# Which DMA queue carries the raw MoE weights during attention, and how the absolute values of a block are spread over slots

## The chip, the cores and the metric

The kernel runs on one core of a Trainium2 chip. The metric is the device time of one execution in microseconds (us); the time of a kernel is the median of several runs.

## What is computed

The reference chains three stages, all in float32 at their ends:

```python
# 1. attention over 2 x 8 heads, 768 tokens, 64 wide: a token sees only tokens of its own cluster
mask = argmax(q_n @ c_n)[:, None] == argmax(k_n @ c_n)[None, :]
attn = softmax(where(mask, scale * q @ k.T, -1e9));  x = concat_heads(attn @ v)      # 1536 x 512
# 2. a dense block of 2048 hidden units; w_in and w_out arrive as float64
h = x @ w_in;  r = maximum(h, 0);  x = (s * r * r + b) @ w_out
# 3. eight experts, top-1 routing
e = argmax(x_n @ en.T / tau);  out = gate[:, None] * (maximum(x @ w1[e], 0) @ w2[e])
```

## The kernel before

Attention runs head by head, sixteen heads. The order of its instructions is written out by hand: every step is entered with a due time by `at(t, f)` (twelve units of due time to a head), the steps are sorted by due time, and `order.pin` keeps that order on all five engines: TensorE (PE), VectorE (DVE), ScalarE (ACT), GpSimd (POOL) and SyncE (SP, which only issues DMAs). So each engine, and the DMA queue that it feeds, meets its instructions in the order of the due times.

For each head, TensorE computes the maxima's scores (`M`, line 223, tile M), which VectorE reduces. `mneg` and `mrow` turn the row maxima of a head into one row: TensorE transposes them (line 235, tile mr), ScalarE copies the row out of PSUM (line 237, tile mrs), and SyncE issues a 3 KB DMA that writes the row into the head's tile qa (line 238, qa<-mrs). The next head's score products (`Sx`, line 247) read that row, so TensorE waits for the DMA before the first of them; ScalarE takes the exponentials (line 249) and TensorE multiplies with v (line 268).

Stage 2 needs w_in and w_out as float32. They arrive as float64 and are converted by bit operations, in 16 blocks f = 0 to 15. `load_f64(f, eng)` issues the two loads of a block, 512 KB each (lines 522 and 523, tile raw), on the queue of the engine `eng`. The tiles raw have six buffers, that is, three blocks. `conv_steps(f)` converts a block in steps: ScalarE takes absolute values of both halves (line 422), VectorE clamps (425), shifts (432) and merges sign and low bits (435 and 437, twice), and the last step issues the load of block f + 3 into the buffers that block f has left (line 441). The steps of blocks 0 to 3 are spread over three heads each, at the due times of `CONV` added to 36 f + 12. The steps of block 4 follow one unit apart from due time 176.2, during the last two heads. Blocks 0 to 2 are loaded at the due times of `FETCH` on ScalarE's queue.

Which block's load goes where, before: block 3 (issued behind the conversion of block 0) on ScalarE's queue; blocks 4, 5, 6 and 7 (issued behind the conversions of blocks 1, 2, 3 and 4) on SyncE's. The loads of blocks 8 to 15 are issued on SyncE's queue in stage 2, whose first chunk converts the remaining blocks.

The load behind the conversion of block f < 4 has due time 36 f + 43.2, which is unit 7.2 of a head. Around it in that head stand: the load of v (due 6), the two conversions of the coming k and q on ScalarE (6 and 8, line 150), the exponentials (7, 8, 9), and `mrow` (8.5).

Of the kernel before, what the change touches and what calls it, by code (L numbers as in the profile page):

```python
# [33 lines left out]
WARM = -26  # L34
HEAT = ((-41, 7), (-30.5, 6), (-22, 6))
SETUP, FETCH = 6.3, (5.3, 17.3, 29.3)
CONV = (3.2, 7.2, 11.2, 15.2, 19.2, 23.2, 27.2, 31.2)
F, DM, TC = 2048, 512, 512
NF, KD, NTT = F // P, DM // P, TC // P
E, F2 = 8, 1024  # L40
NWA = 5
# [339 lines left out]
class Moe:  # L381
# [11 lines left out]
    def hooks(self, ms, mb):  # L393
# [12 lines left out]
        for f in range(NWA):  # L406
            for n, t in enumerate(CONV):
                out.append((36 * f + 12 + t if f < NWA - 1 else 176.2 + n, lambda f=f: next(self.steps(f), None)))
# [7 lines left out]
    def conv_steps(self, f, wide=False):  # L416
        nc = self.nc
        r = self.loaded.pop(f)
        t = self.w32(f, U32)
        u = [self.ps([P, DM], "cv", "ab"[a]).bitcast(U32) if wide else t[:, a] for a in range(2)]  # L420
        for a in range(2):
            nc.scalar.activation(out=t[:, a].bitcast(F32), in_=r[a][:, :, 1].bitcast(F32), func=AF.Abs)
        yield
        s = t.rearrange("p a (w o) -> p o (a w)", o=2)
        nc.vector.tensor_scalar(out=s.bitcast(F32), in0=s.bitcast(F32), scalar1=CLAMP_LO, scalar2=CLAMP_HI, op0=ALU.max, op1=ALU.min)
        yield
        shift = dict(scalar1=5, scalar2=2, op0=ALU.logical_shift_left, op1=ALU.logical_shift_right)
        if wide:
            for a in range(2):
                nc.vector.tensor_scalar(out=u[a], in0=t[:, a], **shift)  # L430
        else:
            nc.vector.tensor_scalar(out=s, in0=s, **shift)
        yield
        for a in range(2):
            nc.vector.scalar_tensor_tensor(out=u[a], in0=r[a][:, :, 1], scalar=0xC0000000, in1=u[a], op0=ALU.bitwise_and, op1=ALU.bitwise_or)
            yield
            nc.vector.scalar_tensor_tensor(out=t[:, a], in0=r[a][:, :, 0], scalar=29, in1=u[a], op0=ALU.logical_shift_right, op1=ALU.bitwise_or)
            yield
        self.wT[f] = t
        if f + 3 < NF:  # L440
            self.loaded[f + 3] = self.load_f64(f + 3, nc.scalar if f + 3 < NWA - 1 else nc.sync)
        yield

    def pools(self):
# [747 lines left out]
```

## Time and profile before

| what | us |
|---|---|
| median of 3 runs | 823.32 |
| lowest and highest of the runs | 821.75, 825.11 |
| the profiled execution's own time | 824.21 |
| its span, first to last instruction | 822.3 |
| mean granted clock of TensorE, share of full speed | 0.967 |

The profile is of one execution. Times in its rows count from the first instruction of the span. A row of the timeline gives the start, the duration, the engine, the source line, the operation, the tile written and the tiles read, and in brackets the idle time of the engine just before it with what ended that. "SPq" and "ACTq" are the issuing queues of SyncE and ScalarE. A row of a window gives the stretch, its length, the busy time of each engine, the granted clock of TensorE and what the DMA engines did.

### The profile page before, as it was taken

What the parts mean: (1) busy time and instruction counts of PE and PEld (TensorE: products, weight loads), DVE (VectorE), ACT (ScalarE), POOL (GpSimd) and SP (SyncE); (2) the same over time, 40 slices, a digit from 0 to 9 for tenths busy, and PEclk for the clock granted to TensorE, in tenths of its full rate; (3) what the DMA queues carried; (4) which work ended last, traced back from release to release, by engine and by line L of the source; (5) the groups of instructions that cost most, each with busy time, mean ns of one, the idle gap of its engine ahead of it and who ended that gap; (6) DMA issues with size and microseconds to landing.
All of it is one profiled execution on the core that took longest, in us unless ns stands there. A gap on an engine that the chain in (4) does not pass through costs nothing. (4 is left out here: it accounts for less than half of the span.)

```text
span 822.3 us, 12229 instructions
## 1 busy us (share of the span) xinstructions
PE 769.7 (94%) x4191; PEld 580.2 (71%) x4193; DVE 526.9 (64%) x1087; ACT 421.6 (51%) x841; POOL 347.5 (42%) x277
## 2 busy tenths in 40 slices
PE   7699999898998889999999999997999999999994
PEld 3456555454554458888778787775879998989883
DVE  5769789695895779994353642648446635756650
ACT  5355465454653665646445554444346645756651
POOL 2067766575674655435434443445032202220000
PEclk9799999998998999999999999989999999999998
DMA  5155423334232205611000042254131844876600
GB/s 147 49 139 175 124 72 92 111 91 119 73 76 63 60 22 170 184 55 52 1 1 1 7 147 86 94 191 142 65 103 58 272 141 157 236 259 228 211 17 23
DMA packets 75470, 88.73 MB, mean 108 GB/s; under 512 B 7445, under 2 KB 58549, under 8 KB 75008
## 3 DMA queue, kind: packets, MB, share of 16 engines
q1 hardware_dynamic: 68704, 69.67, 27.9%
q0 software_dynamic: 4000, 13.90, 5.3%
q10 hardware_dynamic: 2688, 4.19, 1.7%
q8 instruction: 40, 0.66, 0.3%
q14 instruction: 38, 0.31, 0.1%
HBM read 70.57 MB, written 7.34 MB: 95 GB/s over the span
## 5 line engine op out<-in xcount | busy, mean ns | idle before, releaser
L531 POOL TENSOR_TENSOR wl<-w,wh 128x512 fp32r<-128x512 f32 x96 | 123.1, 1307 | 131.5 <-ACT wh L529 128.9
L249 ACT ACTIVATE pt<-S 128x384 f32<-128x384 f32 x192 | 91.6, 490 | 123.1 <-PE S L248 121.0
L224 DVE TENSOR_REDUCE mx<-M 128x1 f32<-128x384 f32 x192 | 101.8, 551 | 54.8 <-PE M L223 52.8
L260 POOL TENSOR_TENSOR acc<-acc,pt 128x768 f32<-128x768 f32 x61 | 106.1, 1740 | 6.5 <-ACT pt L249 4.1
L552 PE MATMUL hp<-x,wh 128*128 128x512 f32 x384 | 107.2, 400 | 0.3 <-ACT wh L529 0.3
L552 PE MATMUL hp<-x,spare 128*128 128x256 f32 x732 | 96.1, 284 | 2.0 <-PEq L984 1.7
L552 PEld LDWEIGHTS hp<-x,spare 128*128 128x128 f32 x732 | 92.7, 190 | 6.9 <-issue 4.1
L560 PE MATMUL y<-wd,gg 128*128 128x512 f32 x360 | 93.2, 395 | 0.0
L608 DVE SCALAR_TENSOR_TENSOR hp<-hp,sb,t 128x512 f32<-128x512 f32 x48 | 36.3, 757 | 78.8 <-ACT t L607 78.8
L247 PE MATMUL S<-qa,ka 97*128 97x384 f32 x192 | 72.5, 377 | 13.2 <-DMA qa<-mrs 11.5
L552 PEld LDWEIGHTS hp<-x,wh 128*128 128x128 f32 x384 | 71.9, 191 | 15.5 <-ACT wh L529 0.9
L223 PE MATMUL M<-ka,qa 80*128 80x384 f32 x192 | 79.0, 412 | 3.6 <-DVE mx L224 2.3
L268 PE MATMUL pv<-pt,vn 128*64 128x385 f32 x384 | 78.8, 534 | 0.0
L560 PE MATMUL y<-wh,gh 128*128 128x512 f32 x192 | 75.6, 394 | 1.7 <-ACT gh L611 1.7
L560 PE MATMUL y<-wl,gh 128*128 128x512 f32 x192 | 75.3, 392 | 0.0
L545 DVE TENSOR_TENSOR wd<-w,wd 128x512 fp32r<-128x512 f32 x64 | 43.3, 686 | 44.4 <-ACT wd L544 41.0
L560 PEld LDWEIGHTS y<-wd,gg 128*128 128x128 f32 x360 | 63.7, 189 | 10.1 <-DVE gg L1081 0.2
L1033 POOL DMA_INDIRECT row<-rows,idx x24 | 28.0, 1166 | 95.7 <-PE tp L1045 50.8
L248 PE MATMUL S<-qb,kb 128*128 128x384 f32 x192 | 66.7, 347 | 0.0
L607 ACT ACTIVATE t<-hp 128x512 f32<-128x512 f32 x48 | 28.7, 598 | 73.9 <-PE hp L552 73.9
L223 PEld LDWEIGHTS M<-ka,qa 80*128 80x128 f32 x192 | 37.1, 193 | 39.2 <-issue 8.2
L560 PE MATMUL y<-wh,gl 128*128 128x512 f32 x192 | 59.4, 391 | 0.0
(269 smaller groups left out, 1371.8 us busy)
## 6 DMA issues: line engine op xcount, KB each, us to landing
w<-in_moe_w_dram SPq DMA_DIRECT2D x128, 256.0 KB
raw<-in_moe_w_in_dram SPq DMA_DIRECT2D x12, 512.0 KB
raw<-in_moe_w_out_dram SPq DMA_DIRECT2D x12, 512.0 KB
qn<-in_q_dram SPq DMA_DIRECT2D x16, 192.0 KB
kn<-in_k_dram SPq DMA_DIRECT2D x16, 192.0 KB
vn<-in_v_dram SPq DMA_DIRECT2D x16, 192.0 KB
ka<-kb SPq DMA_DIRECT2D x16, 192.0 KB
qa<-qb SPq DMA_DIRECT2D x16, 192.0 KB
```

The costliest lines, as they stand in the source:

```text
L223: nc.tensor.matmul(pp, qa[i][0:80, r * P:(r + 1) * P], ka[i][0:80, c * HS:(c + 1) * HS])
L224: nc.vector.tensor_reduce(out=mxt[j % 2][:, r, c:c + 1], in_=pp, axis=AX.X, op=ALU.max)
L247: nc.tensor.matmul(pp, ka[i][0:97, t * P:(t + 1) * P], qa[i][0:97, w], start=True, stop=False)
L248: nc.tensor.matmul(pp, kb[i][:, t * P:(t + 1) * P], qb[i][:, w], start=False, stop=True)
L249: exps.setdefault((j, t), []).append(nc.scalar.activation(out=p[:, c, 0:HS], in_=pp, func=AF.Exp, scale=0.125).ins)
L260: eng.tensor_tensor(out=acc[j][-1], in0=acc[j][-1], in1=p[:, :, 0:HS], op=ALU.add)
L268: together(tc, [lambda c=c: nc.tensor.matmul(pv_t[j][c * 64:c * 64 + 64, :], io_t["v", j][:, t, :], p[:, c, :], start=t == 0, stop=t == NR ...
L531: eng.tensor_tensor(out=wl[:, a], in0=w[:, a], in1=wh[:, a].bitcast(F32), op=ALU.subtract)
L545: eng.tensor_tensor(out=t[:, 1], in0=w[:, a], in1=t[:, 0].bitcast(F32), op=ALU.subtract)
L552: self.nc.tensor.matmul(hp, a[:, k * P:(k + 1) * P], b(k), start=n == 0, stop=n == 3 * KD - 1)
L560: self.nc.tensor.matmul(y[i], (gl if n == 2 else gh)[:, s], wl if n == 1 else wh, start=first and n == 0, stop=last and n == 2)
L608: nc.vector.scalar_tensor_tensor(out=hp, in0=hp, scalar=sb[:, 0:1], in1=t, op0=ALU.mult, op1=ALU.mult)
```

## The change

The last step of a conversion chooses the queue by f instead of by f + 3, so that the loads of blocks 3, 4, 5 and 6 are issued on ScalarE's queue and only that of block 7 on SyncE's, among those issued during attention. The loads of blocks 8 to 15 stay on SyncE's. The two absolute values of a block, which were one step, become two steps; `CONV` gets one more due time, 5.2, for the second one. For block 4, whose steps are one unit apart, every step from the second absolute value on moves by one unit, and its last (the load of block 7) to 184.2.

```diff
-CONV = (3.2, 7.2, 11.2, 15.2, 19.2, 23.2, 27.2, 31.2)
+CONV = (3.2, 5.2, 7.2, 11.2, 15.2, 19.2, 23.2, 27.2, 31.2)
...
         for a in range(2):
             nc.scalar.activation(out=t[:, a].bitcast(F32), in_=r[a][:, :, 1].bitcast(F32), func=AF.Abs)
-        yield
+            yield
...
         if f + 3 < NF:
-            self.loaded[f + 3] = self.load_f64(f + 3, nc.scalar if f + 3 < NWA - 1 else nc.sync)
+            self.loaded[f + 3] = self.load_f64(f + 3, nc.scalar if f < NWA - 1 else nc.sync)
```

(NWA is 5.)

## Rows read from the trace of the kernel before

**Rows 1.** Page, part 1: busy time, share of the span and instructions of each engine.
```profile
PE 769.7 (94%) x4191; PEld 580.2 (71%) x4193; DVE 526.9 (64%) x1087; ACT 421.6 (51%) x841; POOL 347.5 (42%) x277
```

**Rows 2.** Windows of attention and of stage 2's first chunk: stretch, length, busy times, clock, DMA.
```profile
30.00:298.00 268.00, 245.88 (x1302) 145.04 (x1299) 207.81 (x434) 137.38 (x333) 163.38 (x108) 0.94 0.35 95
298.00:386.00 88.00, 87.75 (x386) 72.32 (x387) 74.94 (x121) 53.44 (x78) 47.04 (x36) 1.00 0.31 97
```

**Rows 3.** Timeline, TensorE: score products that waited for qa<-mrs, all five.
```profile
98.37 0.41 PE L247 MATMUL S<-qa,ka 97*128 97x384 f32 x1 [1.64 <-DMA qa<-mrs]
...
148.51 0.41 PE L247 MATMUL S<-qa,ka 97*128 97x384 f32 x1 [3.17 <-DMA qa<-mrs]
...
198.67 0.66 PE L247 MATMUL S<-qa,ka 97*128 97x384 f32 x1 [3.03 <-DMA qa<-mrs]
...
249.50 0.66 PE L247 MATMUL S<-qa,ka 97*128 97x384 f32 x1 [2.72 <-DMA qa<-mrs]
...
278.98 0.41 PE L247 MATMUL S<-qa,ka 97*128 97x384 f32 x1 [0.90 <-DMA qa<-mrs]
```

**Rows 4.** Timeline: issues of raw loads and of qa<-mrs, with mr and mrs before them.
```profile
92.20 0.41 ACTq L522 DMA_DIRECT2D raw<-in_moe_w_in_dram  x1
...
94.34 0.76 SPq L238 DMA_DIRECT2D qa<-mrs  x1
...
141.22 0.22 PE L235 MATMUL mr<-identr,mn 128*6 128x128 f32 x1
...
142.05 0.44 SPq L522 DMA_DIRECT2D raw<-in_moe_w_in_dram  x1
...
192.33 0.45 SPq L522 DMA_DIRECT2D raw<-in_moe_w_in_dram  x1
...
243.33 0.25 ACT L237 ACTIVATE mrs<-mr 6x128 f32<-6x128 f32 x1
243.48 1.35 SPq L522 DMA_DIRECT2D raw<-in_moe_w_in_dram  x1
...
245.48 0.75 SPq L238 DMA_DIRECT2D qa<-mrs  x1
...
277.06 0.73 SPq L238 DMA_DIRECT2D qa<-mrs  x1
```

**Rows 5.** Windows from one mr (line 235) to the next; columns as in Rows 2.
```profile
92.61:110.84 18.23, 16.38 (x87) 9.79 (x85) 11.68 (x27) 9.59 (x24) 10.47 (x8) 0.91 0.43 129
...
126.03:141.22 15.19, 14.84 (x86) 8.98 (x85) 14.21 (x30) 8.43 (x22) 11.14 (x8) 1.00 0.32 84
141.22:161.11 19.89, 16.50 (x86) 9.46 (x85) 11.68 (x27) 9.44 (x24) 10.44 (x8) 0.91 0.42 118
...
191.52:212.29 20.77, 17.53 (x87) 10.20 (x85) 11.68 (x27) 9.56 (x24) 10.43 (x8) 0.84 0.39 112
...
242.68:261.87 19.19, 16.05 (x67) 9.00 (x66) 11.65 (x27) 6.39 (x16) 8.57 (x5) 0.82 0.26 79
261.87:275.00 13.13, 12.63 (x64) 7.43 (x63) 8.05 (x17) 6.28 (x16) 8.57 (x5) 1.00 0.12 32
```

**Rows 6.** Timeline: ScalarE idle after block 1's absolute values; block 1's last merge.
```profile
109.84 0.49 ACT L249 ACTIVATE pt<-S 128x384 f32<-128x384 f32 x1 [1.40 <-PE S L248]
...
135.51 0.68 DVE L437 SCALAR_TENSOR_TENSOR w<-raw,w 128x512 uint32<-128x512 uint32 x1
```

**Rows 7.** Timeline: block 4's conversion near the end of attention, and who waits later.
```profile
275.65 1.25 ACT L422 ACTIVATE w<-raw 128x512 f32<-128x512 f32 x2
276.79 0.25 ACT L237 ACTIVATE mrs<-mr 6x128 f32<-6x128 f32 x1
276.93 0.70 DVE L425 TENSOR_SCALAR w<-w 128x1024 f32<-128x1024 f32 x1 [2.52 <-ACT w L422]
...
291.66 0.87 PE L284 MATMUL su<-acc,ones 128*64 128x384 f32 x4 [1.75 <-DVE xu L303]
```

**Rows 8.** Timeline, ScalarE's queue: the longest issue of a raw load.
```profile
73.78 2.43 ACTq L523 DMA_DIRECT2D raw<-in_moe_w_out_dram  x1
```

## The prediction

> **What bounds the kernel now.** I read the busy times on the page first: TensorE is busy 94% of the span [rows 1], so a change on queues can only be worth what TensorE idles or runs slow because of them. The windows by stage come next [rows 2]: attention (30 to 298 us) has 268.0 us with 245.9 us of TensorE at a granted clock of 0.94, and the first chunk of stage 2 right behind it is solid (87.75 of 88.0 us, clock 1.00). The reader is to see two things there. What attention loses is where this change acts, and what attention gains is handed on in full, since the stage behind it waits for nothing but its start.
>
> Then the list of TensorE's waits on DMAs. There is one kind in attention: the first score product of a head waits for the row qa<-mrs, five times, 11.46 us in all [rows 3]. Four of the five stand in the four heads in which a raw load is issued at unit 7.2; the fifth, 0.90 us, stands next to block 4's conversion. Last the issues [rows 4]: in each of the four heads the 1 MB of a raw block is issued just ahead of the small qa<-mrs (2.1 us in the first, 2.0 in the last), on ScalarE's queue in the first (92.20), on SyncE's in the other three (142.05, 192.33, 243.48).
>
> **What such a load costs.** From one mr to the next takes 15.19 us in a clean head (one row stands; six such lie between 15.18 and 15.21) [rows 5]. With a load it takes 18.23 us in the head with the load on ScalarE's queue, and 19.89, 20.77 and 19.19 us with it on SyncE's. So the first costs 3.04 us, the second 4.70, the third 5.58. The fourth has less work than a clean head, for there are no more heads to prepare: from its stalled product to the next mr it takes 12.37 us (261.87 less 249.50), the third head 13.62 us (212.29 less 198.67) [rows 3, 5], at granted clocks that differ little over the windows (0.82 and 0.84). I take the difference, 1.25 us, off 15.19: clean 13.94, cost 5.25. Its bounds are a clean head of 15.19 (cost 4.00) and the next window's 13.13 (cost 6.06).
>
> Each cost has two parts: the wait itself (1.64, 3.17, 3.03, 2.72 [rows 3]) and a rest (1.40, 1.53, 2.55, 2.53). The rest is the clock. The mean granted clock of these windows is 0.91, 0.91, 0.84, 0.82 against 1.00 in the clean ones [rows 5]: TensorE idles, falls to the lower of its two levels (1.2 instead of 2.4 GHz) and needs a while to be granted the higher again. That while came in two sizes, some 1.4 to 1.5 and some 2.5 us.
>
> **Why the one on ScalarE's queue is cheaper.** Counted from mr, the product would have been ready at 4.12, 4.12, 4.12 and 4.10 us (start less wait less mr, [rows 3, 5]); ScalarE's own issuing therefore didn't make it later. The wait ended 6.17, 6.46, 6.34 and 6.02 us after the first of the two loads was issued [rows 3, 4], whichever queue carried it: the small row lands when the large load is through. What differs is the issue: 0.41 us before mr on ScalarE's queue, 0.83, 0.81 and 0.80 us after it on SyncE's [rows 4, 5], where it stands behind the stores and the load of v. 6.17 - 0.41 - 4.12 = 1.64 us, the wait that is seen.
>
> **The change, part by part.** (a) The loads of blocks 4, 5 and 6 move to ScalarE's queue, at the same unit 7.2 as block 3's, between the same neighbours. So each of the three heads should become like the one at 92.61: 3.04 us instead of 4.70, 5.58 and 5.25, that is 1.66 + 2.54 + 2.21 = 6.41 us less. Of this 1.53 + 1.39 + 1.08 = 4.00 us is wait and the rest is clock. The clock part has bounds: with no drop at all behind the waits the three heads cost 1.64 each and the gain is 15.53 - 4.92 = 10.61 us; with the long drop (2.55) each time they cost 4.19 and it is 2.96 us. I take 1.40, the rest of the very head that is copied. ScalarE could also be held by a buffer that isn't free: block 4's load goes into what block 1 left, whose last merge ended at 136.19 [rows 6], 4.6 us before the place of the load (141.22 - 0.41). No wait there.
>
> (b) SyncE's queue loses three pairs of issues. In these heads qa<-mrs was issued behind them; in the last, the row was ready at 243.58 and was issued at 245.48 [rows 4]. This is contained in (a) and not counted again.
>
> (c) The second absolute value (half of 1.25 us, 0.63 [rows 7]) moves from unit 3.2 to 5.2 in blocks 0 to 3. ScalarE sits idle 1.40 us there, waiting for TensorE [rows 6]. I count nothing: the half fits into that idle time. Without that cover it would cost 0.63 us each, four times; in the old place it can at most have delayed as much, so the same is the bound of a gain.
>
> (d) Block 4's pair at 275.65 stands ahead of the last mrs copy at 276.79 [rows 7]. Split, the copy passes the second half and the 0.90 us wait at 278.98 [rows 3] shrinks by up to 0.6. But VectorE's clamp waits for both halves (2.52 us idle before 276.93), and VectorE's work from there to 291 is what TensorE's sums wait for at 291.66 (1.75 us) [rows 7]. The second half now comes behind copy and exponential, some 0.5 us later. I count 0.3 us lost, with bounds of 0.6 either way. The load of block 7, one unit later on SyncE's queue, is needed only in the chunk behind.
>
> **Sum.** -6.41 + 0.3 = -6.1 us. On the profiled execution's own 824.21 that is 818.1; this execution lies 0.89 us above the median of the runs, so against 823.32 it is **817.2 us**. Its own range, with the fourth head's bounds and (d)'s, is 815.5 to 819.
>
> **Rivals.** (1) The clock. It drops for the long time behind each wait, as in two of four cases: gain 2.96 - 0.3, 820.7 us. For it: two of four; against it: these two followed waits near 3 us, and the wait of 1.64 had the short drop. The opposite, no drops: 813.0 us.
>
> (2) Only issue time is saved. The row goes out sooner and is held by the same load just as long. In the fourth head it would be 1.90 us (243.58 to 245.48, with an issue of 1.35), in the other two, whose first issue took 0.45, an estimated 0.6 each: 3.1 us, less 0.3, 820.5. Against it stands the head at 92.61. The Trainium skill speaks for it: "DMA: Bandwidth & Descriptors", Issuing engines are not separate DMA queues, has all queues run on the same 16 engines and only the sequencer's issuing time saved. The trace agrees as to the transfer (6.0 to 6.5 us on both queues); the earlier place of the issue comes on top of that.
>
> (3) The small row overtakes the load once they stand on different queues. Then the waits vanish with their clock drops, 15.5 us, 808 us. The same page, Queues, rings and completion order, lets each DMA engine alternate between queues packet by packet, which would do this; it also says that a DMA's completion count lands only behind the earlier writes of its engine across queues, which would not. The trace is against overtaking: at 94.34 the row was issued on the other queue and still took until 98.37, 4.03 us, where it took 1.92 (277.06 to 278.98) with no such load near it [rows 3, 4].
>
> (4) **Slower:** ScalarE is held while issuing. One of its eight issues took 2.43 us [rows 8], and in SyncE's queue one took 1.35 [rows 4]. At 73.78 it fell into an idle stretch; at unit 7.2 the exponentials and the mrs copy stand behind it. An issue of 2.43 instead of about 0.46 sends the row out 1.97 us later; with 4.03 us to land, the product starts 7.73 us after mr, against 7.29, 7.15 and 6.82 now, in a longer idle time with the long clock drop: about 1.5 us more a head, 828 us if all three are held. It decides from a hold of about 1.4 us. Against it: the issue at 92.20, in the same place, took 0.41.
>
> (5) It does nothing: the order behind attention, which isn't written by hand, comes out some us worse and eats the gain, 822 to 825.
>
> **How the numbers follow.** Forecast (815.5 to 819) 0.55, fewer drops (down to 812) 0.13, rivals 1 and 2 together (819 to 821.3) 0.20, overtaking 0.03, held issues 0.05, rival 5 0.04. The range 813.0 to 821.0 leaves out the last three and a little of the second and third. A difference of 0.5%, 4.1 us, is about what a measurement of this kernel can tell from none, so faster means under 819.2: 0.55 + 0.13 + 0.03 = 0.71. Within: 0.20 + 0.04 = 0.24. Slower: 0.05.
>
> **What the profile after would show.** Right: three raw issues on ScalarE's queue some 0.4 us before mr; four waits for qa<-mrs near 1.6 us; windows from mr to mr near 18.2 (the fourth near 17.0); the fifth wait under 0.6. Wrong: waits still near 3 us (rival 2), none (3), a raw issue over 1.4 us on ScalarE (4), windows over 19 with short waits (1), or heads as forecast and a late start of stage 2 (d, 5).

## The result, and the profile after

The median falls from 824.75 us (818.25 to 826.92, measured beside it) to **815.92 us** (814.10 to 821.52). The ratio of the runs is 0.9913, with a 95% interval of 0.9894 to 0.9931, that is 5.7 to 8.7 us less. The forecast was 817.2 us, a gain of 6.1. The profiled execution of the changed kernel took 815.01 us against 824.21, with a span of 813.1 against 822.3 and a mean granted clock of 0.976 against 0.967.

TensorE's busy time, to compare with [rows 1], is 5.9 us smaller with the same work, and the rest of the 9.2 us by which the spans differ is idle time:

```profile
PE 763.8 (94%) x4193; PEld 577.3 (71%) x4193; DVE 526.5 (65%) x1087; ACT 421.7 (52%) x841; POOL 347.6 (43%) x277
```

The list of TensorE's waits of the kernel after: engine, tile and line, who released it; us in all, times, longest. The five waits for the row were 11.5 us together [rows 3].

```profile
PE S L247 <- DMA qa<-mrs: 7.6, 5, 2.0
```

The timeline of the kernel after: each raw load of the four heads with its mr, two issues of the row, and the five score products that waited (in brackets the wait). They answer to [rows 3, 4].

```profile
91.99 0.41 ACTq L522 DMA_DIRECT2D raw<-in_moe_w_in_dram  x1
92.40 0.22 PE L235 MATMUL mr<-identr,mn 128*6 128x128 f32 x1
94.14 0.76 SPq L238 DMA_DIRECT2D qa<-mrs  x1
98.07 0.41 PE L247 MATMUL S<-qa,ka 97*128 97x384 f32 x1 [1.54 <-DMA qa<-mrs]
...
140.47 0.40 ACTq L522 DMA_DIRECT2D raw<-in_moe_w_in_dram  x1
140.89 0.22 PE L235 MATMUL mr<-identr,mn 128*6 128x128 f32 x1
146.74 0.42 PE L247 MATMUL S<-qa,ka 97*128 97x384 f32 x1 [1.75 <-DMA qa<-mrs]
...
187.64 0.41 ACTq L522 DMA_DIRECT2D raw<-in_moe_w_in_dram  x1
188.06 0.22 PE L235 MATMUL mr<-identr,mn 128*6 128x128 f32 x1
189.79 0.77 SPq L238 DMA_DIRECT2D qa<-mrs  x1
194.21 0.66 PE L247 MATMUL S<-qa,ka 97*128 97x384 f32 x1 [2.03 <-DMA qa<-mrs]
...
238.15 0.41 ACTq L522 DMA_DIRECT2D raw<-in_moe_w_in_dram  x1
238.56 0.22 PE L235 MATMUL mr<-identr,mn 128*6 128x128 f32 x1
244.50 0.41 PE L247 MATMUL S<-qa,ka 97*128 97x384 f32 x1 [1.85 <-DMA qa<-mrs]
...
272.12 0.41 PE L247 MATMUL S<-qa,ka 97*128 97x384 f32 x1 [0.44 <-DMA qa<-mrs]
```

All four loads are now issued 0.41 or 0.42 us ahead of mr. The waits of the second to fourth fall from 3.17, 3.03 and 2.72 to 1.75, 2.03 and 1.85 us. The windows from one mr to the next (columns as in [rows 2]) answer to [rows 5]:

```profile
92.40:110.53 18.13, 16.38 (x87) 9.74 (x85) 11.69 (x27) 9.58 (x24) 10.47 (x8) 0.91 0.42 129
125.71:140.89 15.18, 14.82 (x86) 8.98 (x85) 14.24 (x30) 8.42 (x22) 11.17 (x8) 1.00 0.33 84
140.89:157.65 16.76, 14.80 (x86) 8.96 (x85) 11.67 (x27) 9.45 (x24) 10.46 (x8) 1.00 0.47 141
188.06:208.17 20.11, 17.86 (x86) 10.31 (x85) 11.68 (x27) 9.57 (x24) 10.43 (x8) 0.83 0.39 115
238.56:255.59 17.03, 14.78 (x66) 8.30 (x65) 11.64 (x27) 6.33 (x16) 8.55 (x5) 0.90 0.29 89
```

The reader is to see that the gain is spread unevenly: 19.89 to 16.76, 20.77 to 20.11, 19.19 to 17.03, that is 3.13, 0.66 and 2.16 us, **5.95 us** in the three heads. The head at 92.40, which the change leaves alone, gives 0.10, and the clean heads are as long as before. The wait of 1.75 us left the clock at 1.00 over its window, the wait of 2.03 took it to 0.83. The stretch of 5.93 us from the waiting product on, in the second to the fourth head, shows it from nearby (the clock is the third figure from the end):

```profile
146.74:152.67 5.93, 5.72 (x34) 3.75 (x35) 2.88 (x6) 2.83 (x8) 2.84 (x2) 1.00 0.22 51
194.21:200.14 5.93, 5.93 (x20) 3.04 (x20) 1.77 (x4) 1.36 (x3) 2.51 (x2) 0.50 0.20 47
244.50:250.43 5.93, 5.93 (x24) 3.17 (x24) 2.46 (x6) 1.26 (x3) 0.00 (x0) 0.71 0.07 17
```

At 0.50 the engine stood at the lower of its two levels, 1.2 GHz, all the way and issued 20 matmuls; at 1.00 it issued 34 in the same time.

**Where the rest of the profiled difference lies.** Stage 2's first product marks the end of attention. It starts at 298.08 us before and at 291.92 after, 6.16 us earlier; these are its rows, before and then after:

```profile
298.08 1.20 PE L552 MATMUL hp<-x,wh 128*128 128x512 f32 x4 [0.28 <-ACT wh L529]
```

```profile
291.92 1.18 PE L552 MATMUL hp<-x,wh 128*128 128x512 f32 x4 [0.54 <-ACT wh L529]
```

The spans differ by 9.2 us, so 3.0 us more were lost later in the execution profiled before. Windows of the same two stretches of stage 2, 222 us behind its start, show most of it: the clock is 0.89 and 0.94 before, 1.00 after.

```profile
520.00:540.00 20.00, 17.61 (x82) 13.23 (x81) 12.66 (x43) 6.49 (x9) 9.61 (x8) 0.89 0.30 98
540.00:560.00 20.00, 20.00 (x84) 16.39 (x84) 8.44 (x9) 11.88 (x21) 11.18 (x11) 0.94 0.66 234
```

```profile
514.00:534.00 20.00, 17.62 (x90) 13.40 (x89) 13.38 (x44) 7.15 (x10) 10.00 (x8) 1.00 0.29 93
534.00:554.00 20.00, 20.00 (x89) 16.25 (x87) 10.62 (x13) 10.89 (x20) 12.84 (x11) 1.00 0.74 263
```

I don't count this as an effect of the change. From stage 2's start to the end of the span takes 524.2 us before, 521.2 after, and between 521.0 and 523.9 in the seven experiments below, in no order that follows their edits. So a single profiled execution scatters by some 3 us there, and attention's 6.16 us is the part that the trace ties to the change.

### The profile page after: what moved, and what is told of

It is laid out like the page before. It is cut to its first block, busy times and chain, and to the rows that moved or that the text cites. A ratio compares the mean times of both kernels' runs of the same rounds, so it can differ in the third digit from the quotient of the medians.

```text
span 813.1 us, 12238 instructions
## 1 busy us (share of the span) xinstructions
PE 763.8 (94%) x4193; PEld 577.3 (71%) x4193; DVE 526.5 (65%) x1087; ACT 421.7 (52%) x841; POOL 347.6 (43%) x277
## 5 line engine op out<-in xcount | busy, mean ns | idle before, releaser
L268 PE MATMUL pv<-pt,vn 128*64 128x385 f32 x384 | 77.1, 525 | 0.0
```

Source lines behind the costliest of these rows:

```text
L268: together(tc, [lambda c=c: nc.tensor.matmul(pv_t[j][c * 64:c * 64 + 64, :], io_t["v", j][:, t, :], p[:, c, :], start=t == 0, stop=t == NR ...
```

## The experiments

My theory after the result: the row lands when the load issued ahead of it is through, so the wait is set by **when** the load is issued relative to mr and by how many bytes it has, and not by which queue carries it. Rivals: ScalarE's queue itself helps (the row isn't behind the load in its own queue), the split of the absolute values has a share, or a later place does as well.

The times, each kernel beside the kernel before on the same chip:

| kernel | runs | median, us | ratio to before, 95% interval |
|---|---|---|---|
| after | 16 | 815.92 | 0.9913 (0.9894 to 0.9931) |
| queue choice alone | 10 | 817.42 | 0.9936 (0.9899 to 0.9973) |
| split absolute values alone | 10 | 821.72 | 1.0021 (0.9977 to 1.0065) |
| SyncE, early | 4 | 803.02 | 0.9790 (0.9718 to 0.9861) |
| ScalarE, early | 4 | 804.14 | 0.9803 (0.9731 to 0.9874) |
| ScalarE, late | 8 | 820.03 | 0.9978 (0.9931 to 1.0025) |
| ScalarE, second half late | 2 | 805.90 | 0.9807 (0.9718 to 0.9897) |
| SyncE, between stores and v | 8 | 819.48 | 0.9956 (0.9919 to 0.9993) |

**The two parts apart.** The first kernel is the kernel before with the new choice of the queue alone:

```diff
-            self.loaded[f + 3] = self.load_f64(f + 3, nc.scalar if f + 3 < NWA - 1 else nc.sync)
+            self.loaded[f + 3] = self.load_f64(f + 3, nc.scalar if f < NWA - 1 else nc.sync)
```

> The queue alone: the loads of blocks 4, 5 and 6 on ScalarE's queue, the two absolute values in one step as in the kernel before. Theory (place of the issue): the waits for qa<-mrs in the four heads with a load lie between 1.5 and 2.1 us, as in the kernel after, the fifth wait (block 4's pair) stays at 0.9; the gain is nearly whole, 6 to 9 us under the kernel before. Rival (the split of the absolute values carries part of it): under 4 us.

The second is the kernel before with the split alone:

```diff
-CONV = (3.2, 7.2, 11.2, 15.2, 19.2, 23.2, 27.2, 31.2)
+CONV = (3.2, 5.2, 7.2, 11.2, 15.2, 19.2, 23.2, 27.2, 31.2)
...
-        yield
+            yield
```

> The split of the absolute values alone; the loads of blocks 4, 5, 6 stay on SyncE's queue. Theory: waits of 1.6, 3.1, 3.0 and 2.7 us as before, the fifth under 0.6; the time within 1 us of the kernel before. Rival: each half moved out of unit 3.2 gives back up to 0.63 us, 2 to 3 us faster.

Measured: 0.9936 and 1.0021. The first is 5.3 us less than the kernel before (2.2 to 8.3), a little under the 6 to 9 that I expected, and its interval overlaps that of the kernel after. The second holds no change. The two intervals just miss each other (0.9973 and 0.9977), so the times already put the gain on the queue choice, though not to a microsecond; the traces show the path. With the queue choice alone the four waits are 1.48, 1.71, 2.00 and 1.91 us, as in the kernel after; its windows show the clock's chance again, this time in the first and third head without a drop (the fourth, not shown, has 0.82):

```profile
97.07:113.56 16.49, 14.80 (x86) 8.98 (x85) 11.67 (x27) 9.44 (x24) 10.48 (x8) 1.00 0.47 142
143.95:162.22 18.27, 16.35 (x86) 9.73 (x85) 11.66 (x27) 9.54 (x24) 10.44 (x8) 0.91 0.42 129
192.58:209.63 17.05, 14.84 (x87) 8.99 (x86) 11.70 (x27) 9.46 (x24) 10.44 (x8) 1.00 0.46 136
```

With the split alone the waits stay those of the kernel before in kind: 1.45 on ScalarE's queue, 3.16, 1.85 and 2.94 on SyncE's, with the loads issued 0.82 us behind mr. Only the fifth, next to block 4's conversion, falls from 0.90 to 0.44, and what follows that (below) gives no more. So the queue choice carries the gain. The 1.85, where I expected 3.0, is a miss for a fixed landing time: this product started 5.14 us after its load's issue, where the others with the whole block ahead took 5.8 to 6.6 unless an issue was held.

**The place instead of the queue.** In both next kernels the last step of the conversion comes at 29.3 instead of 31.2, between the score products and the stores of a head, 3.65 to 3.9 us ahead of mr. One leaves all these loads on SyncE's queue, the other on ScalarE's; the split stays.

```diff
-CONV = (3.2, 5.2, 7.2, 11.2, 15.2, 19.2, 23.2, 27.2, 31.2)
+CONV = (3.2, 5.2, 7.2, 11.2, 15.2, 19.2, 23.2, 27.2, 29.3)
...
-            self.loaded[f + 3] = self.load_f64(f + 3, nc.scalar if f < NWA - 1 else nc.sync)
+            self.loaded[f + 3] = self.load_f64(f + 3, nc.sync)
```

(The second of the two has the first line of this alone.)

> All four loads (blocks 3 to 6) on SyncE's queue, but at unit 5.3 of the head instead of 7.2, ahead of the stores of xt and the load of v: about 3.7 us before mr instead of 0.8 behind it. Theory (only the time of the issue counts; the row lands some 6.2 us after the load was issued, that is 2.5 us behind mr, and the product is ready 4.1 behind it): no wait for qa<-mrs in these four heads, windows from mr to mr of 15.2 (the fourth 13.9), 15 to 19 us under the kernel before, 806 to 810. Rival (a row on the same queue as a large load is held by it, ScalarE's queue is what helps): waits of 2 us and more, time between the two kernels.

> The same early place, unit 5.3, on ScalarE's queue. Theory: the same as with SyncE's queue, no waits, 806 to 810, within 1 us of it. Rival (queue): better than SyncE's queue at the same place by the full wait, or, if ScalarE is held at issuing there (one issue of 2.43 us stood at this unit in the kernel before), worse by 1 to 2 us a head.

Measured: 803.02 and 804.14 us, below the 806 to 810 that I expected. By their ratios they lie some **16 to 17 us below the kernel before** (the intervals reach from 10 to 23) **and 9 to 10 below the kernel after**, on either queue. By the profile no score product of these four heads waits for the row in either (one, on ScalarE's queue, idles 0.17 us, put down to ScalarE's pt); of the kind only the fifth, 0.44 and 0.45 us, is left. The timeline of the one on SyncE's queue, with its load, the stores and the load of v that now follow it, and the row:

```profile
88.73 0.59 SPq L522 DMA_DIRECT2D raw<-in_moe_w_in_dram  x1
...
90.75 1.78 SPq L311 DMA_DIRECT2D xt<-xu  x3
92.38 0.22 PE L235 MATMUL mr<-identr,mn 128*6 128x128 f32 x1
92.57 0.58 SPq L123 DMA_DIRECT2D vn<-in_v_dram  x1
93.72 0.76 SPq L238 DMA_DIRECT2D qa<-mrs  x1
```

Its windows from mr to mr, three of the heads with a load; the clock is 1.00 in all four:

```profile
137.98:153.14 15.16, 14.79 (x86) 8.93 (x85) 11.67 (x27) 9.64 (x24) 10.45 (x8) 1.00 0.42 118
183.52:198.72 15.20, 14.84 (x86) 8.94 (x85) 11.69 (x27) 9.66 (x24) 10.46 (x8) 1.00 0.41 115
229.09:242.42 13.33, 12.94 (x66) 7.78 (x65) 11.61 (x27) 6.37 (x16) 8.56 (x5) 1.00 0.21 69
```

Two things follow. The load itself costs the heads next to nothing where the row doesn't meet it. It moves partly ahead of mr and partly behind it; in the two early kernels the windows behind mr last 15.16 to 15.21 us in the first three heads and those ahead of it 15.18 to 15.21, but for one of 15.43. And the last row gives the clean length of the fourth head, which I had to estimate: 13.33 us. Against clean heads the four loads cost 3.04 + 4.70 + 5.58 + 5.86 = 19.18 us before and 2.94 + 1.57 + 4.92 + 3.70 = 13.13 after; stage 2's start moves by 298.08 - 278.7 = 19.4 us in this kernel.

**Places close to mr, on the other queue each.** One kernel issues on ScalarE's queue behind mr (last step 32.4), the other on SyncE's, between the stores of a head and the load of v (29.7). Both keep the split.

```diff
-CONV = (3.2, 5.2, 7.2, 11.2, 15.2, 19.2, 23.2, 27.2, 31.2)
+CONV = (3.2, 5.2, 7.2, 11.2, 15.2, 19.2, 23.2, 27.2, 32.4)
```

> All four loads on ScalarE's queue, but at unit 8.4, right ahead of the mrs copy: about 0.9 us behind mr, where SyncE's queue issued them in the kernel before. Queue as in the kernel after, time of issue as in the kernel before. Theory (time of issue): waits for qa<-mrs of about 3 us in all four heads (0.9 + 6.2 - 4.1), time as the kernel before or up to 4 us above it, since block 3's head loses too. Rival (queue): waits of 2.0 us or less, time as the kernel after.

```diff
-CONV = (3.2, 5.2, 7.2, 11.2, 15.2, 19.2, 23.2, 27.2, 31.2)
+CONV = (3.2, 5.2, 7.2, 11.2, 15.2, 19.2, 23.2, 27.2, 29.7)
...
-            self.loaded[f + 3] = self.load_f64(f + 3, nc.scalar if f < NWA - 1 else nc.sync)
+            self.loaded[f + 3] = self.load_f64(f + 3, nc.sync)
```

> All four loads on SyncE's queue at unit 5.7, between the stores of xt and the load of v: about 0.2 us behind mr, between ScalarE's place (0.41 ahead) and SyncE's (0.8 behind). Theory: waits near 2.3 us in all four heads (0.2 + 6.2 - 4.1), 816 to 823. Rival (queue): waits as in the kernel before, near 3 us, 825 and more.

Measured: 820.03 and 819.48. The first kernel missed the place that it was built for: its loads were issued 0.36 us behind mr and not 0.9, so waits of 3 us weren't put to the test on ScalarE's queue, and its time isn't above that of the kernel before. In the second the place came out, and the waits lie a little under the 2.3 us expected, but for one. The load and the waiting product of the second head, on ScalarE's queue and then on SyncE's (their mr at 142.58 and 141.27):

```profile
142.95 0.39 ACTq L522 DMA_DIRECT2D raw<-in_moe_w_in_dram  x1
148.77 0.66 PE L247 MATMUL S<-qa,ka 97*128 97x384 f32 x1 [2.08 <-DMA qa<-mrs]
```

```profile
141.46 0.59 SPq L522 DMA_DIRECT2D raw<-in_moe_w_in_dram  x1
147.55 0.41 PE L247 MATMUL S<-qa,ka 97*128 97x384 f32 x1 [2.16 <-DMA qa<-mrs]
```

Sorted by the place of the issue, over all traces, the waits of the four heads are:

| issue from mr, us | queue | waits, us |
|---|---|---|
| -3.9 | ScalarE | none |
| -3.65 | SyncE | none |
| -0.41 | ScalarE | 1.45 to 2.03, mean 1.74 (ten heads) |
| +0.19 | SyncE | 2.00, 2.16, 1.98; 2.95 with a held issue |
| +0.36 | ScalarE | 2.11, 2.08, 2.19; 2.62 with a held issue |
| +0.82 | SyncE | 3.17, 3.03, 3.16, 1.85; 2.72, 2.94 with a held issue |

At nearly the same place, +0.19 and +0.36, the waits without a held issue agree within some 0.2 us although in one kernel the row stands behind the load in the same queue and in the other it doesn't. With the early pair this leaves nothing for the queue beyond the place that it gives. (At 0.41 us ahead of mr only ScalarE's queue was measured, at 0.82 behind it only SyncE's.) The Trainium skill bears on it ("DMA: Bandwidth & Descriptors", Issuing engines are not separate DMA queues): DMAs of different issuing engines run on the same 16 DMA engines. These rows agree.

The traces also keep each DMA packet with its queue, size, start and length, though no view prints them. The row goes out as six packets of 512 bytes, and in every head in which a product waited for it behind such a load, the product started 0.59 to 0.93 us after the last of the six had ended. In the 24 heads with a whole block ahead, that last packet ended between 1.08 us before and 0.58 us after the last packet of the load; it came before it in five of the 14 heads with the load on the other queue and in five of the 10 with both on one. So "the row lands when the load is through" holds to about a microsecond on either queue, and not strictly. One late packet of the six makes much of the scatter at +0.82: with the wait of 3.16 us five had ended 4.7 us after the load's issue and the sixth at 5.8; with the wait of 1.85 all six had ended at 4.5.

A held issue comes on top of the place, on either queue. In the fourth head the second issue of the load took 1.89 us in the kernel on SyncE's queue, and the row went out only at 242.44, 3.28 us behind mr (239.16):

```profile
239.34 0.59 SPq L522 DMA_DIRECT2D raw<-in_moe_w_in_dram  x1
239.97 1.89 SPq L523 DMA_DIRECT2D raw<-in_moe_w_out_dram  x1
241.91 0.43 SPq L123 DMA_DIRECT2D vn<-in_v_dram  x1
242.44 0.75 SPq L238 DMA_DIRECT2D qa<-mrs  x1
```

In the late kernel on ScalarE's queue the same issue took 1.20 us and stood ahead of the mrs copy. Their waits, 2.95 and 2.62 us, are 0.4 to 1.0 longer than the other three of the same kernel. This is rival 4 of the prediction in kind, seen where the load stands behind mr and not in the kernel after. At +0.82 a hold of 1.35 or 1.48 us did no such thing: those two waits are shorter than three of the four beside them.

**Half the bytes ahead.** Here the first 512 KB stay at unit 7.2 and the second are issued at unit 10.2, behind the row; all on ScalarE's queue. (`load_f64` gets a part number, and `CONV` one more due time, 34.2.)

```diff
-            self.loaded[f + 3] = self.load_f64(f + 3, nc.scalar if f < NWA - 1 else nc.sync)
+            eng = nc.scalar if f < NWA - 1 else nc.sync
+            n = self.load_f64(f + 3, eng, 0)
+        yield
+        if f + 3 < NF:
+            self.loaded[f + 3] = self.load_f64(f + 3, eng, 1, n)
```

> As the kernel after, but only the first 512 KB of a block (w_in) is issued at unit 7.2; the second (w_out) comes at unit 10.2, behind the issue of qa<-mrs. Same queue and same bytes. Theory (the row waits for what was issued ahead of it): half the bytes are through about 3 us after the issue, before the product is ready; waits under 0.5 us, windows of 15.2 to 15.7, 803 to 808. Rival (the row shares the DMA engines with all that is in flight, later issues too): waits of 1 us and more, 810 and more.

Measured: 805.90 us. The timeline of two heads' first load (line 527 here), the first head's row and second load (529), and the waiting products:

```profile
93.61 0.41 ACTq L527 DMA_DIRECT2D raw<-in_moe_w_in_dram  x1
95.35 0.76 SPq L238 DMA_DIRECT2D qa<-mrs  x1
97.32 0.33 ACTq L529 DMA_DIRECT2D raw<-in_moe_w_out_dram  x1
98.71 0.42 PE L247 MATMUL S<-qa,ka 97*128 97x384 f32 x1 [0.57 <-ACT kb L168]
...
139.58 0.41 ACTq L527 DMA_DIRECT2D raw<-in_moe_w_in_dram  x1
144.42 0.41 PE L247 MATMUL S<-qa,ka 97*128 97x384 f32 x1 [0.31 <-DMA qa<-mrs]
```

The product starts 5.10, 4.84 and 5.05 us after the first load's issue in the three heads in which it waited (0.57, 0.31 and 0.55 us, two of them a little over the 0.5 expected; the first is put down to ScalarE's kb, but in a clean head, as at 92.38 in the early kernel on SyncE's queue, the same product starts at 96.35, ahead of the kb at 96.48, so I read it as the row too). In the remaining head it starts 4.76 us after the issue and idles 0.22, put down to ScalarE's pt. With the whole block ahead it was 6.08, 6.27, 6.57 and 6.35 in the kernel after. So with 512 KB fewer ahead of it the row lands about 6.32 - 5.00 = 1.3 us sooner, and the 512 KB issued behind it don't give that back. A part of this may be the row's own issue, which ScalarE's shorter issuing brought forward from 1.73 to 1.34 us behind mr; in the packets of the kernel after, the second 512 KB end 1.25 to 1.69 us behind the first. The clock stays at 1.00 in all four windows. The Trainium skill's page "SBUF — State Buffer" (The DMA setup-cost knee) has a fit for one transfer: about 2 us and the bytes at 436 GB/s. The estimate from its second part for 512 KB is 1.2 us, which this difference agrees with.

## Why the prediction was right, step by step

**The bound.** Right. What attention gained was handed on in full: stage 2 starts 6.16 us earlier, and nothing behind it took that back.

**The wait and what sets it.** Right in kind: it is the issue of the load relative to mr. The waits came out at 1.75, 2.03 and 1.85 where the copy of the first head gave 1.64 for each. The step that was too smooth is the landing time: 6.08 to 6.57 us after the issue in the kernel after, and 5.1 to 6.9 over all kernels with a whole block ahead, where four rows between 6.02 and 6.46 had looked like a constant. The wait parts of the three heads fell by 1.42 + 1.00 + 0.87 = 3.29 us, not 4.00.

**The clock term.** Right in sum by a mean, wrong head by head. I gave each head the rest of the one that it copies, 1.40 us. The three heads show -0.18, 2.89 and, by the clean 13.33 us, 1.85. That the long drop belongs to waits near 3 us, which I held against rival 1, has fallen. For waits of 1.45 to 2.19 us in the heads of 15.19 us, cost less wait over all traces shown or told of here comes in three sizes: about -0.15 in five heads (windows at clock 1.00), 1.36 to 1.43 in six (0.91), 2.69 to 2.94 in four (0.83). The length of the wait doesn't sort them: 2.16 us had no drop and 1.98 the long one. Their mean is 1.26 us, so 1.40 was a good price for a sum over many heads and none for a single one. With three heads it was in part luck: their clock parts come to 4.56 us where I had 4.20, and with such sizes three heads could give anything from about -0.5 to 8.4.

**The fourth head.** Mis-sized: I took 13.94 us as its clean length from the stretches behind two stalled products, as if the clock had taken the same from both. It is 13.33, inside the bounds I gave. So its cost was 5.86 before, where I had 5.25, and 3.70 after, where I had 3.04; the two errors cancel, and the difference is 2.16 against 2.21.

**The sum of (a).** -5.95 us against -6.41. In the order of its terms: waits 0.71 us less gained than forecast, clock 0.25 more (2.66 against 2.41).

**(c), the split in blocks 0 to 3.** Counted at nothing; the clean heads last 15.18 to 15.21 us as before, and the split alone gives no gain that could be measured.

**(d), the end of attention.** The path was seen rightly. The timeline of ScalarE after, which answers to [rows 7]: the copy passes the second half. Its last row is the product of TensorE that waits for VectorE.

```profile
269.36 0.68 ACT L422 ACTIVATE w<-raw 128x512 f32<-128x512 f32 x1
269.93 0.25 ACT L237 ACTIVATE mrs<-mr 6x128 f32<-6x128 f32 x1
...
270.46 0.65 ACT L422 ACTIVATE w<-raw 128x512 f32<-128x512 f32 x1
...
285.29 0.87 PE L284 MATMUL su<-acc,ones 128*64 128x384 f32 x4 [2.26 <-DVE xu L303]
```

The fifth wait shrinks from 0.90 to 0.44. VectorE's clamp starts 2.43 us after the last mr instead of 1.93, half a microsecond later as forecast, and the wait of TensorE's sums grows from 1.75 [rows 7] to 2.26. So 0.46 us is gained and 0.51 lost, a loss of 0.05 where I had 0.3. In all seven kernels with the split the sums wait 2.24 to 2.26 us, in the two without it 1.74 and 1.75. The whole stretch from the last mr to stage 2 (23.08 us before, 23.21 after) lies between 22.5 and 23.4 over the other kernels and can't show so little.

**The rivals.** (2), only issue time saved, falls by the waits: in the second and third head the row went out only 0.19 and 0.18 us sooner behind mr, but the waits fell by 1.42 and 1.00. In the fourth it went out 1.48 us sooner and was held 0.60 longer, so there the gain of 0.87 is issue time, as this rival says, and less than its 1.90. (3), overtaking, falls twice: by the waits that are left, and by the row's waits on one or two queues, which agree. The row did end ahead of the load's last packet in some heads, but no more often on two queues than on one. Of the packet by packet arbitration that the Trainium skill describes ("DMA: Bandwidth & Descriptors", Queues, rings and completion order) no run here shows a benefit for a small transfer issued behind a large one. (4) didn't decide: no raw issue in these heads took over 0.47 us on ScalarE's queue in the trace after. (5) didn't come. (1) came in one head of three, its opposite in another.

**What the prediction didn't see.** Its own rows said more: with a landing of about 6.2 us and the product ready 4.12 us after mr, a load issued more than 2.1 us ahead of mr makes no wait at all, on either queue. Its trace even had such a load: the one of [rows 8], whose first half was issued 3.95 us ahead of mr on ScalarE's queue, is followed by no wait in [rows 3]. The change moved the loads from 0.8 us behind mr to 0.4 ahead; the whole 16 to 17 us lay another 3 us further on.

**Left open.** Why one of the row's six packets comes late in some heads and not in others, with the same bytes ahead; what decides whether the clock drops behind a wait of 1.5 to 2.2 us; and whether the row would be held as long if it were issued on ScalarE's queue itself, which wasn't tried.

## What to carry to other kernels

When a small transfer that the critical engine needs stands behind a bulk load, place the load by time: early enough that it is through when the small one goes out, or with part of it behind; which engine issues it mattered here only by the place it gave. Price a wait of TensorE as the wait and, on average over heads, the clock behind it (1.26 us here on waits of 1.45 to 2.19), and give the range both ends. And work out from the same rows at what place the wait would vanish before sizing a change that only shortens it.

## What the runs showed of the hardware that was not expected

- Waits of nearly equal length had unequal prices: 2.16 us cost 2.00 us of the window with no clock drop, 1.98 us cost 4.75 with a long one, in one and the same execution (the kernel with the loads between stores and v).
- 1 MB of load inside a head cost next to nothing in itself: in the two early kernels the first three windows from mr last 15.16 to 15.21 us with it; the clean windows between such heads last 15.16 to 15.22 over all kernels.
- An issue of a raw load in these heads took 0.33 to 0.76 us but in four cases, 1.20 to 1.89 us (in the kernel before 1.35 [rows 4]). All four fell in the fourth head with the load issued behind mr; in none of these heads with the load ahead of mr did one take over 0.60. The one of 2.43 us [rows 8] is of an earlier head.
